# Padding the r and k loads of a fused RWKV-and-FFN kernel to all partitions, with changes to its order of loads and its schedule

## The chip, the cores and the metric

The kernel runs on one core of a Trainium2 chip. The metric is the device time of one execution in microseconds (us), median of several runs. Every run named here was in the fast state (granted TensorE clock 0.98 to 1.00 of full speed on average). A profiled span runs from the first to the last instruction and came out 1 to 2 us below the time of the same run; I compare spans with spans and medians with medians.

Engines: PE is TensorE's matmuls, PEld its weight loads, DVE is VectorE, ACT is ScalarE, POOL is GpSimd, SP issues the loads. All kernel operations go through one helper, so nearly every line of the profile says L91, and tiles are what identifies an operation.

## The reference, cut to what matters

```python
batch, n_heads, seq, head_dim = (4, 8, 768, 48)
for t in range(S):                              # RWKV5, per head
    cur = np.einsum('bhd,bhe->bhde', u[None] * kt, vt)
    y[:, :, t] = np.einsum('bhd,bhde->bhe', rt, state + cur)
    state = w[None, :, :, None] * state + np.einsum('bhd,bhe->bhde', kt, vt)
x = y.transpose(0, 2, 1, 3).reshape(3072, 384)
xn = x / np.sqrt(np.mean(x * x, axis=-1, keepdims=True) + 1e-06) * rms_g
g = xn @ w_gate                                 # 384 x 1536
silu = g * (1.0 / (1.0 + np.exp(-g)))
out = (silu * (xn @ w_val)) @ w_out             # 1536 x 384
```

Everything from `r`, `k` and `v` is float32; the three weight matrices arrive as float64.

## The kernel before

The recurrence is cut into 12 blocks of 64 tokens. In a block, r and k are scaled by powers of w (DVE, "decay"), multiplied into scores (PE), masked, multiplied with v, and added to the state's contribution. The block's output is normalised and goes through the two gated products and the output product. Blocks 0 and 1 use the weights while they are still being loaded as 64-bit pieces (`raw`) and converted by ACT, DVE and POOL into `wa`, `wb`, `wo`. Later blocks run in pairs and need seven products instead of eight for a group, for which sums of weight halves (`s1`, `s2`, `s4`) and of tokens (`t`) must exist.

The tile `chan` (called `CH` in the code) holds r and k of one block with channels in the partitions: two heads of 48 channels, one at rows 0 to 47, one at rows 64 to 111. Only block 0's host array carried the zero rows between them, so all other blocks were loaded in two halves:

```python
def load_chan(s):
    if s == 0:
        sp.dma_start(out=CH, in_=chan_0)
        return
    for z in range(2):
        sp.dma_start(out=CH[64 * z : 64 * z + D], in_=chan[s, z])
```

What happens at the start is laid out by a list scheduler. Each operation is entered with its engine, an estimated cost, and what it reads and writes. A random search over goals picks an order, which every engine then executes as a fixed program. Stretches where PE has nothing to do in the beginning are filled with products of a constant tile (`warm`, called filler below), which are meant to keep PE's clock up. In the trace of this kernel the granted clock is 1.00 in the first 20 us, and 0.50 from 28.6 to 35.4 us, around the end of a gap of 5.73 us in PE's work. The code:

```python
add("DVE", 0.12 + 0.55 * n, ["up"] + keys("CHr"), keys("MEr", "MEt"),
    lambda part=part: decay_r(s, *part), port=True, name=f"R {s}")
...
def warm(us):
    for _ in range(int((us - 0.3) / 0.22)):
        pe.matmul(gv["c"][:, 0, 0:P], ones, ones, start=True, stop=True)

p.run(cells, 25.0, {"PE": 1.5, "DVE": 1.5, "ACT": 3.0, "POOL": 6.3, "SP": 1.7}, warm)
```

The first pair of blocks (2 and 3) makes the remaining sums between its own products; `(m, k)` is the product after which DVE does the add:

```python
if first_block:
    fill.update({(0, 0): lambda: token_sum(s, 3)})
    fill.update({(0, 1): lambda: token_sum(s, 4)})
    fill.update({(1, 0): lambda: unit_sum(1, 1), (2, 0): lambda: unit_sum(2, 1)})
    fill.update({(2, 1): lambda: unit_sum(4, 1), (2, 4): lambda: unit_sum(3, 1)})
```

Of the kernel before, what the change touches and what calls it, by code (L numbers as in the profile page):

```python
# [49 lines left out]
P = 128  # L50
# [10 lines left out]
B, H, S, D = 4, 8, 768, 48  # L61
HP = H // 2
L = 64
NS = S // L
# [29 lines left out]
class Plan:  # L94
# [28 lines left out]
    def schedule(self, goals, free):  # L123
# [34 lines left out]
                    ready[self.ops[j][0]].add(j)  # L158
        return start

    def run(self, cells, first, free, idle=None, trials=3000):



        goals, t = {}, first
        for i in cells:
            goals[i] = t
            t += self.ops[i][1]
        rng, best = random.Random(2), None
        for trial in range(trials):  # L170
            new = dict(goals)
            if trial and rng.random() < 0.5:
                a, by = rng.randrange(len(cells)), rng.uniform(-15, 15)
                for i in cells[a : a + 1 + int(rng.expovariate(1 / 6))]:
                    new[i] += by
            elif trial:
                new[rng.randrange(len(self.ops))] = rng.uniform(0, t)
            start = self.schedule(new, free)
            end = max(start[i] + self.ops[i][1] for i in cells) + 0.3 * sum(start[i] for i in cells) / len(cells)
            if best is None or end <= best[0]:  # L180
                best, goals = (end, start), new
        self.start = best[1]
        busy = free["PE"]
        for i in sorted(range(len(self.ops)), key=lambda i: (self.start[i], i)):
            if self.ops[i][0] == "PE":
                if idle and busy < first:
                    idle(self.start[i] - busy)
                busy = self.start[i] + self.ops[i][1]
            self.ops[i][3]()


@with_exitstack
def fast(ctx, tc, chan, tok, vpad, wka, wkb, wot, cols, u_row, chan_0, out, bad):




# [7 lines left out]
    PIECE = NQ * CC * P  # L205
# [15 lines left out]


    col = c_tile([P, 2 * HP + CC], "col")
    act.dma_start(out=col, in_=cols)
    wraw, ucol, gcol = col[:, 0:HP], col[:, HP : 2 * HP], col[:, 2 * HP :]
    utab = c_tile([P, HP, D], "utab")
    eps = c_tile([P, 1], "eps")
# [85 lines left out]


    def load_chan(s):
        if s == 0:
            sp.dma_start(out=CH, in_=chan_0)
            return
        for z in range(2):
            sp.dma_start(out=CH[64 * z : 64 * z + D], in_=chan[s, z])  # L320

    def load_tok(s):
        sp.dma_start(out=TOK, in_=tok[s])
# [11 lines left out]
    wa = [c_tile([P, NQ, CC, P], f"wa_{i}") for i in range(WQ)]  # L335
    wb = [c_tile([P, NQ, CC, P], f"wb_{i}") for i in range(WQ)]
    wo = [c_tile([P, NQ, DM], f"wo_{i}") for i in range(WQ)]
    CUT, N_RAW, N_BITS = PIECE // 2, 6, 3
    raw_of = [raws.tile([P, CUT], I64, name=f"raw_{i}") for i in range(N_RAW if wide else 0)]
    bits_of = [raws.tile([P, CUT], I32, name=f"bits_{i}") for i in range(N_BITS if wide else 0)]  # L340
    ulp_of = [raws.tile([P, CUT], I32, name=f"ulp_{i}") for i in range(N_BITS if wide else 0)]
# [2 lines left out]
    def piece(p, dst, src, key, lo, size):  # L344



        n = n_pieces[0]
        n_pieces[0] += 1
        flat = free_dims(dst, (1, PIECE))[:, lo : lo + size]  # L350
        part = src[:, lo : lo + size]
        share = size / 576
        if not wide:
            p.add("SP", 0.8 * share, [], [key, "rounded"], lambda: sp.dma_start(out=flat, in_=part), land=2)
            return
        raw, bits, ulp = raw_of[n % N_RAW][:, 0:size], bits_of[n % N_BITS][:, 0:size], ulp_of[n % N_BITS][:, 0:size]
        r, b, u = f"raw{n % N_RAW}", f"bits{n % N_BITS}", f"ulp{n % N_BITS}"
        words = raw.bitcast(I32).rearrange("p (n z) -> p n z", z=2)
        hi, lower = words[:, :, 1], words[:, :, 0].bitcast(U32)
        p.add("SP", 1.35 * share, [], [r], lambda: sp.dma_start(out=raw, in_=part), land=1.8, name=f"load {n}")  # L360
        p.add(
            "ACT", 0.1 + 0.64 * share, [r], [u],
            lambda: act.activation(ulp, lower, AF.Copy, scale=2.0**-29), name=f"ulp {n}",
        )
        p.add(
            "DVE", 0.07 + 0.38 * share, [r], [b],
            lambda: dve.tensor_scalar(
                out=bits, in0=hi, scalar1=3, scalar2=0x3FFFFFF8, op0=ALU.logical_shift_left, op1=ALU.bitwise_and
            ),
            port=True, name=f"bits1 {n}",  # L370
        )
        p.add(
            "DVE", 0.07 + 0.69 * share, [r, b], [b],
            lambda: dve.scalar_tensor_tensor(
                out=bits, in0=hi, scalar=-0x40000000, in1=bits, op0=ALU.bitwise_and, op1=ALU.bitwise_or
            ),
            port=True, name=f"bits2 {n}",
        )
        p.add(
            "POOL", 0.15 + 1.3 * share, [b, u], [key, "rounded"],  # L380
            lambda: pool.tensor_tensor(out=flat.bitcast(I32), in0=bits, in1=ulp, op=ALU.add), port=True,
            name=f"sum {n}",
        )
# [209 lines left out]
    p = Plan()  # L593
# [12 lines left out]
        i = turn["at"] % 2  # L606
        return at[i], f"at{i}"

    add("SP", 0.0, [], ["w"], lambda: None, land=2.4)
    add("DVE", 2.4, ["w"], ["pw"], powers, name="powers")  # L610
    add("DVE", 0.43, ["pw"], ["up"], lambda: dve.tensor_mul(up, pw, by_inv), port=True)
    add("DVE", 0.43, ["pw"], ["down"], lambda: dve.tensor_mul(down, pw_rev, by_inv), port=True)
# [9 lines left out]
    add("ACT", 3.0, ["pw"], ["khd"], state_decay, name="khd")  # L622

    def loads(s):
        add("SP", 2.3 if s == 0 else 1.8, [], ["CHr0", "CHr1", "CHk0", "CHk1"], lambda: load_chan(s), land=1.6)
        add("SP", 1.8, [], ["TOKr", "TOKk"], lambda: load_tok(s), land=1.8)
        add("SP", 1.6, [], ["VSv"], lambda: load_v(s), land=1.8)
        if s == 0:
            add("SP", 0.5, [], ["utab"], load_u, land=1.8)

    def mixing(s):
        quick = s == 0
# [181 lines left out]
    for n, reads, writes in (  # L814
        (1, ["wa2.0", "wa2.1", "wb2.0", "wb2.1"], ["s1"]), (2, ["s1", "wa0.0", "wa0.1", "wa0.2"], ["s2"]),
    ):
        add("DVE", 1.25, ["sums"] + reads, writes, lambda n=n: unit_sum(n, 0), port=True, name=f"sum {n}")
    cell(1, 3)
    for n, reads, writes in (
        (4, ["s2", "wb0.0", "wb0.1", "wb0.2"], ["s4"]), (3, ["wa0.0", "wa0.1", "wa0.2"], ["wa2.0", "wa2.1"]),  # L820
# [10 lines left out]
        for _ in range(int((us - 0.3) / 0.22)):  # L831
            pe.matmul(gv["c"][:, 0, 0:P], ones, ones, start=True, stop=True)

    p.run(cells, 25.0, {"PE": 1.5, "DVE": 1.5, "ACT": 3.0, "POOL": 6.3, "SP": 1.7}, warm)


    def at_bank(name):
# [154 lines left out]
    for s in range(FIRST, NS, 2):  # L992
        first_block, n = s == FIRST, s + 2
        fill = {}
        if first_block:
            fill.update({(0, 0): lambda: token_sum(s, 3)})
            fill.update({(0, 1): lambda: token_sum(s, 4)})
            fill.update({(1, 0): lambda: unit_sum(1, 1), (2, 0): lambda: unit_sum(2, 1)})
            fill.update({(2, 1): lambda: unit_sum(4, 1), (2, 4): lambda: unit_sum(3, 1)})
        if n < NS:  # L1000
            plan = {
                (0, 2): "R", (1, 1): "K", (1, 4): "1", (2, 0): "2", (2, 2): "3d", (3, 0): "h", (3, 2): "D",
                (3, 5): "aAm", (4, 1): "M", (4, 2): "H", (4, 4): "yY", (5, 3): "q",
            }
        else:
            plan = {}
        look = {(m, k) for m in range(NN // 2) for k in (2, 5) if m != 2}
        if first_block:
            look = {(m, k) for m, k in look if k == 5 or m == 4}
        elif n == NS:  # L1010
            look |= {(2, 2), (2, 5), (5, 6)}
        for m in range(NN // 2):
            steps = group(s, m)
            for k, f in enumerate(steps):
                f()
                if (m, k) in fill:
                    fill[m, k]()
                if (m, k) in plan:
                    mix(n, plan[m, k])
                if (m, k) in look:  # L1020
                    check()
        if n == NS:
            break
        mix(n, "uU"), mix(n + 1, "R123")
        project(s, 0, False), mix(n, "r"), mix(n + 1, "KdD")
        project(s, 0, True), mix(n + 1, "aA"), mix(n, "n")
        project(s, 1, False), mix(n + 1, "mMh")
        project(s, 1, True), mix(n + 1, "yYH")
        project(s, 2, False), mix(n + 1, "q")
        project(s, 2, True), mix(n + 1, "r")  # L1030
        project(s, 3, False), mix(n + 1, "n")
        project(s, 3, True), mix(n + 1, "uU")
        for x in (1, 2, 3, 4):
            token_sum(n, x)
# [424 lines left out]
@with_exitstack  # L1459
def program(ctx, tc, fast_args, general_args, w, u, out):  # L1460
    nc = tc.nc
    flags = ctx.enter_context(tc.tile_pool(name="flags", bufs=1))
    bad = flags.tile([1, 1], I32, name="bad")
    chan, tok, vpad, wka, wkb, wot, cols, u_row, chan_0 = fast_args
    n_bad = fast(tc, chan, tok, vpad, wka, wkb, wot, cols, u_row, chan_0, out, bad)
    with tc.If(n_bad > 0):
        rT, kT, k, v, w_gate, w_val, w_out, rms_g = general_args
        general(tc, rT, kT, k, v, w, u, w_gate, w_val, w_out, rms_g, out)
# [67 lines left out]
```

## Time and profile before

| what | value |
|---|---|
| time, median of 3 runs | 663.31 us (663.28 to 663.75) |
| first product with a weight (`first_a<-xa,wa`) on PE | 35.28 us |
| first product of the paired blocks (`a<-xa,wa`) | 162.24 us |
| first product of the last output group (`po`) | 623.41 us |

The three starts cut the span into stages. First the head of the page, with the span and each engine's busy time, share and count of instructions.

```profile
span 662.2 us, 15313 instructions
PE 640.5 (97%) x6534; PEld 506.8 (77%) x6534; DVE 385.9 (58%) x560; ACT 341.0 (52%) x952; POOL 44.6 (7%) x39
```

PE is busy for 97% of the span. That average hides what this PE time is: some of the first 35 us is filler. So the busy share says that PE is the bound, but not that nothing can be saved. The stages in the prediction answer that. The second place with idle PE time is the first paired block. The list of waits from 150 to 205 us shows it (columns: engine and tile that waited, engine and tile waited for, total us, times, longest).

```profile
PE b L91 <- DVE gv L91: 1.9, 3, 1.0
PE a L91 <- DVE h L91: 1.3, 1, 1.3
```

PE waits 3.2 us there, always for DVE, which is where the three adds stood that the change moves.

### The profile page before, as it was taken

How to read it: one execution, taken by the hardware profiler on the slowest of the kernel's cores; microseconds unless marked ns; L12 is line 12 of the kernel's file. 1: busy time of each engine (PE TensorE's matmuls, PEld its weight loads, DVE VectorE, ACT ScalarE, POOL GpSimd, SP SyncE). 2: the span in 40 equal slices, each digit the busy share in tenths (PEclk: the TensorE clock that was granted, in tenths of full speed). 3: DMA queues.
4: the chain of work that ended last, by engine and by line, in shares of the span. 5: the costliest groups of instructions: out<-in, count | busy, mean ns of one | idle time of the engine just before them, and what ended most of it. 6: DMA issues, size and time to landing. Idle time of an engine off the chain costs nothing.

```text
span 662.2 us, 15313 instructions
## 1 busy us (share of the span) xinstructions
PE 640.5 (97%) x6534; PEld 506.8 (77%) x6534; DVE 385.9 (58%) x560; ACT 341.0 (52%) x952; POOL 44.6 (7%) x39
## 2 busy tenths in 40 slices
PE   9699999999989999999999999999999999999996
PEld 8586788786868866888866888866888866788753
DVE  5688688854876653576562577572566571555400
ACT  5388248734354573555673555582555492434400
POOL 3044523200000000000000000000000000000000
PEclk9898999999999999999999999999999999999999
DMA  9688636061205232314333314334323321122111
GB/s 281 154 183 296 192 117 172 1 139 47 63 19 118 83 67 76 91 37 97 112 82 89 81 46 87 103 79 113 73 55 75 112 62 29 38 72 73 54 27 28
DMA packets 20078, 61.61 MB, mean 93 GB/s; under 512 B 3072, under 2 KB 6272, under 8 KB 18816
## 3 DMA queue, kind: packets, MB, share of 16 engines
q1 hardware_dynamic: 19856, 60.53, 34.5%
q8 instruction: 53, 0.87, 0.6%
q14 instruction: 25, 0.20, 0.1%
q10 hardware_dynamic: 144, 0.01, 0.0%
HBM read 55.81 MB, written 4.72 MB: 91 GB/s over the span
## 4 chain that ended last, share of the span: by engine, by line
PE 84%; ACT 6%; DVE 4%; DMA 3%; issue 2%; POOL 0%; SPq 0%; DVEq 0%; ACTq 0%; POOLq 0%
PE po L91 24%; PE b L91 15%; PE a L91 10%; PE c L91 9%; PE first_b L91 5%; PE first_c L91 4%; PE first_a L91 4%; PE at L91 4%; PE py L91 3%; PE pa L91 2%; PE pu L91 2%; DMA chan<-in_chan_dram 2%; ACT MO L91 2%; ACT ME L91 1%; DVE gv L91 1%
## 5 line engine op out<-in xcount | busy, mean ns | idle before, releaser
L91 PE MATMUL po<-wo,h 128*128 128x384 f32 x480 | 159.8, 489 | 0.8 <-DVE bad L91 0.8
L91 PEld LDWEIGHTS po<-wo,h 128*128 128x128 f32 x480 | 90.0, 190 | 60.2 <-PE pc L91 0.8
L91 DVE TENSOR_TENSOR gv<-b,m 128x512 f32<-128x512 f32 x90 | 62.0, 689 | 79.4 <-PE b L91 76.0
L91 ACT ACTIVATE gv<-gv 128x512 f32<-128x512 f32 (+1 forms) x60 | 30.9, 518 | 51.5 <-DVE gv L91 51.5
L91 ACT ACTIVATE ME<-dmask,du 64x64 f32<-64x64 f32 x176 | 43.7, 329 | 12.3 <-DVE du L91 11.9
L91 DVE TENSOR_TENSOR gv<-c,gv 128x512 f32<-128x512 f32 x60 | 41.4, 690 | 14.4 <-PE c L91 13.3
L91 ACT COPY o<-po 128x384 f32<-128x384 f32 x20 | 9.5, 474 | 77.4 <-PE po L91 39.3
L91 PE MATMUL a<-xa,wa 64*128 64x256 f32 x360 | 45.0, 382 | 1.9 <-DVE h L91 1.9
L91 PE MATMUL b<-xa,wa 64*128 64x256 f32 x360 | 44.6, 380 | 1.6 <-DVE gv L91 1.6
L91 ACT ACTIVATE MO<-dmask,du 64x64 f32<-64x64 f32 x176 | 44.4, 334 | 0.4
L91 PE MATMUL b<-t,wb 64*128 64x256 f32 x360 | 44.4, 379 | 0.0
L91 PE MATMUL c<-xb,s 64*128 64x256 f32 x360 | 44.3, 378 | 0.0
L91 PE MATMUL b<-t,s 64*128 64x256 f32 x360 | 44.0, 377 | 0.3 <-DVE gv L91 0.3
L91 PE MATMUL c<-t,s 64*128 64x256 f32 x360 | 43.9, 376 | 0.0
L91 PE MATMUL a<-xb,wb 64*128 64x256 f32 x360 | 43.9, 376 | 0.0
L91 ACT ACTIVATE mag<-again 128x288 f32<-128x288 f32 x48 | 22.1, 461 | 35.9 <-DMA again<-in_wot_dram 14.6
L91 PEld LDWEIGHTS a<-xa,wa 64*128 64x128 f32 x360 | 33.8, 187 | 8.3 <-DVE h L91 4.1
L91 PEld LDWEIGHTS b<-xa,wa 64*128 64x128 f32 x360 | 34.1, 187 | 7.6 <-DVE gv L91 4.0
L91 PEld LDWEIGHTS b<-t,s 64*128 64x128 f32 x360 | 34.8, 187 | 4.6 <-DVE gv L91 0.7
L91 PEld LDWEIGHTS c<-t,s 64*128 64x128 f32 x360 | 34.9, 187 | 4.0
L91 PEld LDWEIGHTS a<-xb,wb 64*128 64x128 f32 x360 | 34.9, 187 | 4.0
L91 PEld LDWEIGHTS b<-t,wb 64*128 64x128 f32 x360 | 34.4, 187 | 4.4 <-DVE gv L91 0.3
(146 smaller groups left out, 1095.8 us busy)
## 6 DMA issues: line engine op xcount, KB each, us to landing
TOK<-in_tok_dram SPq DMA_DIRECT2D x12, 768.0 KB, 4.9
chan<-in_chan_dram SPq DMA_DIRECT2D x22, 384.0 KB, 6.4
VS<-in_vpad_dram SPq DMA_DIRECT2D x24, 336.0 KB, 4.9
raw<-in_wot_dram SPq DMA_DIRECT2D x8, 576.0 KB, 4.1
out_dram<-o SPq DMA_DIRECT2D x48, 96.0 KB, 2.2
again<-in_wka_dram SPq DMA_DIRECT2D x16, 288.0 KB, 3.1
again<-in_wkb_dram SPq DMA_DIRECT2D x16, 288.0 KB, 2.8
again<-in_wot_dram SPq DMA_DIRECT2D x16, 288.0 KB, 2.8
```

The source lines that it names most:

```text
L91: return lambda *args, **kwargs: self.tc.keep_in_program_order(give(*args, **kwargs))
```

## The change

The intent has four parts: load r and k of every block over all 128 partitions; bring the small `col` table and block 0's k ahead of other loads; let the search judge an order with later landing times (`LAND` 2.1 us, a `replay` with longer costs, another seed); and make three of the sums inside the plan instead of in the first paired block. The diff, cut to its core:

```diff
     def load_chan(s):
-        if s == 0:
-            sp.dma_start(out=CH, in_=chan_0)
-            return
-        for z in range(2):
-            sp.dma_start(out=CH[64 * z : 64 * z + D], in_=chan[s, z])
+        sp.dma_start(out=CH, in_=chan[s])
 ...  (host)
-    chan_0 = np.zeros((2, 64) + chan.shape[3:], np.float32)
-    chan_0[:, 0:D] = chan[0]
+    chan = np.pad(chan, [(0, 0), (0, 0), (0, 64 - D)] + [(0, 0)] * 4).reshape((NS, P) + chan.shape[3:])
 ...  (first loads)
-    act.dma_start(out=col, in_=cols)
+    sp.dma_start(out=col, in_=cols)
 ...
         if s == 0:
-            add("SP", 0.5, [], ["utab"], load_u, land=1.8)
+            for i, x in ((1, "k"), (0, "r")):
+                add(
+                    "SP", 1.2, [], [f"CH{x}0", f"CH{x}1"],
+                    lambda i=i: sp.dma_start(out=CH[:, i], in_=chan[s, :, i]), land=LAND, name=f"load {x} {s}",
+                )
 ...  (the search)
-        rng, best = random.Random(2), None
+        rng, best = random.Random(3), None
 ...
-            end = max(start[i] + self.ops[i][1] for i in cells) + 0.3 * sum(start[i] for i in cells) / len(cells)
+            end = self.replay(start, free)
+            end = max(end[i] for i in cells) + 0.3 * sum(end[i] for i in cells) / len(cells)
 ...  (the plan)
+    for n, reads, writes in (
+        (1, ["wa3.0", "wa3.1", "wb3.0", "wb3.1"], ["s1'"]), (2, ["s1'", "wa1.0", "wa1.1"], ["s2'"]),
+        (4, ["s2'", "wb1.0", "wb1.1"], ["s4'"]),
+    ):
+        add("DVE", 1.25, ["sums"] + reads, writes, lambda n=n: unit_sum(n, 1), port=True, name=f"sum {n}'")
 ...  (first paired block)
-            fill.update({(1, 0): lambda: unit_sum(1, 1), (2, 0): lambda: unit_sum(2, 1)})
-            fill.update({(2, 1): lambda: unit_sum(4, 1), (2, 4): lambda: unit_sum(3, 1)})
+            fill.update({(2, 4): lambda: unit_sum(3, 1)})
```

More of the change, by code (lines that the diff above doesn't have):

```diff
@@ L159, in schedule, with replay @@
         return start
+    def replay(self, start, free):
+        free, port, end = dict(free), {"DVE": 0.0, "POOL": 0.0}, [0.0] * len(self.ops)
+        for i in sorted(range(len(self.ops)), key=lambda i: (start[i], i)):
+            e, cost, deps, _, _, locks, _ = self.ops[i]
+            s = max([free[e]] + [end[d] + self.hop(d, i) + (1.0 if self.ops[d][0] == "SP" else 0.05) for d in deps])
+            if locks:
+                s = max(s, port["POOL" if e == "DVE" else "DVE"])
+            free[e] = end[i] = s + cost * (1.0 if e == "PE" else 1.05)
+            if locks:
+                port[e] = end[i]
+        return end
     def run(self, cells, first, free, idle=None, trials=3000):
@@ L192, in fast @@
 @with_exitstack
-def fast(ctx, tc, chan, tok, vpad, wka, wkb, wot, cols, u_row, chan_0, out, bad):
+def fast(ctx, tc, chan, tok, vpad, wka, wkb, wot, cols, u_row, out, bad):
     nc = tc.nc
@@ L337, in fast @@
     wo = [c_tile([P, NQ, DM], f"wo_{i}") for i in range(WQ)]
-    CUT, N_RAW, N_BITS = PIECE // 2, 6, 3
+    CUT, N_RAW, N_BITS, LAND = PIECE // 2, 6, 3, 2.1
     raw_of = [raws.tile([P, CUT], I64, name=f"raw_{i}") for i in range(N_RAW if wide else 0)]
@@ L353, in piece @@
         if not wide:
-            p.add("SP", 0.8 * share, [], [key, "rounded"], lambda: sp.dma_start(out=flat, in_=part), land=2)
+            p.add("SP", 0.7 * share, [], [key, "rounded"], lambda: sp.dma_start(out=flat, in_=part), land=LAND)
             return
@@ L359, in piece @@
         hi, lower = words[:, :, 1], words[:, :, 0].bitcast(U32)
-        p.add("SP", 1.35 * share, [], [r], lambda: sp.dma_start(out=raw, in_=part), land=1.8, name=f"load {n}")
+        p.add("SP", 1.35 * share, [], [r], lambda: sp.dma_start(out=raw, in_=part), land=LAND, name=f"load {n}")
         p.add(
@@ L607, in next_at @@
         return at[i], f"at{i}"
-    add("SP", 0.0, [], ["w"], lambda: None, land=2.4)
+    add("SP", 0.3, [], ["w"], lambda: None, land=1.9)
     add("DVE", 2.4, ["w"], ["pw"], powers, name="powers")
@@ L624, in loads @@
     def loads(s):
-        add("SP", 2.3 if s == 0 else 1.8, [], ["CHr0", "CHr1", "CHk0", "CHk1"], lambda: load_chan(s), land=1.6)
-        add("SP", 1.8, [], ["TOKr", "TOKk"], lambda: load_tok(s), land=1.8)
-        add("SP", 1.6, [], ["VSv"], lambda: load_v(s), land=1.8)
         if s == 0:
-            add("SP", 0.5, [], ["utab"], load_u, land=1.8)
+            for i, x in ((1, "k"), (0, "r")):
[3 more added lines that the diff above has]
+                )
+        else:
+            add(
+                "SP", 2.4, [], ["CHr0", "CHr1", "CHk0", "CHk1"], lambda: load_chan(s), land=LAND, name=f"load chan {s}"
+            )
+        add("SP", 1.8, [], ["TOKr", "TOKk"], lambda: load_tok(s), land=LAND, name=f"load tok {s}")
+        add("SP", 3.2, [], ["VSv"], lambda: load_v(s), land=LAND, name=f"load v {s}")
+        if s == 0:
+            add("SP", 0.5, [], ["utab"], load_u, land=LAND)
     def mixing(s):
@@ L832, in warm @@
             pe.matmul(gv["c"][:, 0, 0:P], ones, ones, start=True, stop=True)
-    p.run(cells, 25.0, {"PE": 1.5, "DVE": 1.5, "ACT": 3.0, "POOL": 6.3, "SP": 1.7}, warm)
+    p.run(cells, 25.0, {"PE": 1.5, "DVE": 1.5, "ACT": 2.5, "POOL": 6.3, "SP": 1.8}, warm)
     def at_bank(name):
@@ L1463, in program @@
     bad = flags.tile([1, 1], I32, name="bad")
-    chan, tok, vpad, wka, wkb, wot, cols, u_row, chan_0 = fast_args
-    n_bad = fast(tc, chan, tok, vpad, wka, wkb, wot, cols, u_row, chan_0, out, bad)
+    chan, tok, vpad, wka, wkb, wot, cols, u_row = fast_args
+    n_bad = fast(tc, chan, tok, vpad, wka, wkb, wot, cols, u_row, out, bad)
     with tc.If(n_bad > 0):
@@ L1505 @@
         "u_row": c(u.reshape(HP, 2, D).transpose(1, 0, 2).reshape(2, HP * D)),
-        "chan_0": chan_0.reshape((P,) + chan.shape[3:]),
         "rT": c(r.transpose(0, 1, 3, 2)),
@@ L1527 @@
             tc,
-            [args[n] for n in ("chan", "tok", "vpad", "wka", "wkb", "wot", "cols", "u_row", "chan_0")],
+            [args[n] for n in ("chan", "tok", "vpad", "wka", "wkb", "wot", "cols", "u_row")],
             [args[n] for n in ("rT", "kT", "k", "v", "w_gate", "w_val", "w_out", "rms_g")],
```

## The prediction

> **What bounds the kernel now.** I read the stages first: busy time of each engine in stretches of the span. Columns are stretch, then busy us and instructions of PE, PEld, DVE, ACT, POOL, then granted clock, DMA share and GB/s.
>
> ```profile
> 0.00:10.00 10.00, 8.84 (x85) 8.65 (x86) 3.41 (x22) 4.51 (x10) 5.16 (x13) 1.00 0.82 220
> 10.00:20.00 10.00, 9.31 (x212) 8.52 (x214) 9.71 (x15) 6.09 (x16) 0.00 (x0) 1.00 1.06 329
> 20.00:30.00 10.00, 4.27 (x40) 3.94 (x35) 4.29 (x8) 2.69 (x7) 0.21 (x1) 0.93 0.49 110
> ...
> 160.00:200.00 40.00, 36.79 (x373) 30.86 (x373) 28.69 (x40) 19.43 (x58) 0.00 (x0) 1.00 0.18 44
> 200.00:300.00 100.00, 99.81 (x1046) 78.55 (x1044) 58.32 (x82) 53.31 (x155) 0.00 (x0) 1.00 0.32 78
> ```
>
> From 60 to 155 us, and from 200 us on, PE has no gap worth having (99.8 of 100 us): the bound there is PE work, which the change leaves as it is. Only two places hold recoverable time: the start, where no weight product can run before the first token block is ready (the first `first_a<-xa,wa` starts at 35.28 us; much of the PE time before it is filler on `ones`), and 160 to 200 us, where PE lacks 3.2 us. Whatever the start loses, the end loses, since PE is full afterwards.
>
> Next the timeline of 20 to 31 us (start, duration, what, idle before and its releaser).
>
> ```profile
> 21.98 1.58 PE L91 MATMUL first_c<-ones 128*128 128x128 f32 x12
> 25.79 1.22 DVE L91 TENSOR_TENSOR ME<-chan,up 128x1024 f32<-128x1024 f32 x1 [5.24 <-DMA chan<-in_chan_dram]
> ...
> 27.10 1.04 ACT L91 COPY MO<-ME 64x1024 f32<-64x1024 f32 x1 [5.52 <-DVE ME L91]
> ...
> 28.17 0.26 ACT L91 ACTIVATE ms<-at,eps 128x2 f32<-128x2 f32 x1
> 28.46 0.17 DVE L91 RECIPROCAL ms<-ms 128x2 f32<-128x2 f32 x1
> 28.66 0.48 DVE L91 TENSOR_SCALAR diag<-ident,ms 128x128 f32<-128x128 f32 x2
> ...
> 29.29 1.19 PE L91 MATMUL at<-diag,ones 128*128 128x256 f32 x2 [5.73 <-DVE diag L91]
> ...
> 30.52 0.95 DVE L91 TENSOR_TENSOR xa<-yT_first,at 128x768 f32<-128x768 f32 x1 [0.91 <-PE at L91]
> ```
>
> The normalisation of block 0 needs nothing from block 1, but on ACT its square root (28.17) stands behind the copy of block 1's r, and on DVE its reciprocal stands behind block 1's decay. Both therefore wait for block 1's `chan` load. The chain of work that ended last says how long that load took, and which load started everything:
>
> ```profile
> 0.81 6.14 DMA col<-in_cols_dram
> ...
> 14.98 10.68 DMA chan<-in_chan_dram
> ```
>
> Last, what the DMA engines moved in 15 to 17 us (full-height weight loads) and in 19 to 21 us (the 48-row `chan` load):
>
> ```profile
> DMA packets 295, 0.81 MB, mean 404 GB/s; under 512 B 32, under 2 KB 32, under 8 KB 295
> ```
>
> ```profile
> DMA packets 57, 0.34 MB, mean 172 GB/s; under 512 B 12, under 2 KB 12, under 8 KB 17
> ```
>
> DMA is about 100% busy in both, at 404 and 172 GB/s (142 in 21 to 23 us). Same engines, less than half the rate: rows reached, not bytes, set the time.
>
> [...] block 0's `chan` (1 MB, 2.6 us at 404 GB/s) took 5.9 us to land, interleaved with others. [...]after PE's 5.73 us gap the granted clock is 0.50 in 30 to 35 us.
>
> **The change part by part.**
>
> *Order.* Comparing the built programs, DVE, ACT and POOL have the same compute order until about 58 us of the old time (ACT only loses the issue of `col`), and PE swaps only a filler and two weight products. The new random search alters the order from there to the end of the plan, where PE was full before. So the start changes through the data's arrival times.
>
> *First loads.* `col` (5.5 KB) goes from ACT's queue, where its packets shared engines with 1 MB of `chan` and landed at 6.96, to the head of SP's queue. [...]Then k, then r, half of `chan` each: at 404 GB/s about 1.3 us apiece, landing about 5 and 6.3 (the whole was in by 6.8 before). DVE's powers took 6.98 to 9.78 until `up` was ready; now about 3.5 to 6.3, so the first decay starts near 6.4 against 9.81: DVE gains about 3 us. ACT gains about 2 (its k copies start at 5 against 6.98), and hands block 0's scores to PE about 1.7 us sooner. DVE then ends its `KH` pair near 17.5 against 20.55. Alone this is worth nothing: DVE would just wait longer for `chan`.
>
> *Block 1's load.* In the new SP order it stands behind four raw weight pieces, not six (2 x 393 KB less, 1.95 us at 404 GB/s). Before, its bytes started to flow at about 17.4, so now at 15.4. It carries 1.05 MB, not 0.79[...]: 2.6 us at 404 GB/s, to 18.0[...]: 19.8 against 25.66. That is later than the 17.5 where DVE is free, so DMA remains the releaser with some 2 us of wait, and the gain here is 25.79 - 19.8 = **6.0 us**.
>
> *From there to the first weight product.* Decay, copy, root, reciprocal, diag and spread take the same durations, so the first `xa` starts near 24.5 minus half a microsecond. PE's gap shrinks to about 3 us (its filler ends some 3 us sooner, the spread comes 6 us sooner), so its clock may stay up: the spread then takes about 0.6, not 1.19, and the 64 state matmuls 1.6, not 2.80. Since ACT has to evict them before its 8 us of diagonals, I add **1.0 us** (0 if the clock falls, 1.5 if it holds throughout). Block 1's tok data come right behind: 18.0 + 1.95 for two pieces + 1.95 = 21.9, landed by 24, just in time. After this, compute follows compute (ACT diagonals, conversion, silu), and the whole stretch to 58 us moves with it. Sum at the start: **7.0 us**.
>
> *Sums of the other half.* Three adds of 1.34 us leave groups 0 to 2 of the first paired block. There DVE is in arrears: PE waited 1.02 (after `s<-s,wa` and TOK), 1.32 (diagonals late because `du` stood behind `s<-wb,s`), 0.30 and 0.57 us, together 3.2. One of four adds, into `wa`, stays. I give back 2.8 of the 3.2. In the plan the adds fall into 120 to 160 us, where DVE is busy 23.5 of 40 us; in 140 to 160 only 8 of 20. I charge 0.3 for a product delayed by one. Net **2.5 us**.
>
> *Later loads.* The other `chan` loads save a DMA issue each and move a third more bytes, but were hidden: PE is 99.8% busy there. Worth 0.
>
> Sum: 7.0 + 2.5 = 9.5; 663.3 - 9.5 = **653.8 us**, 1.4% faster.
>
> **The rivals.** (1) *The start gains the full DVE head start and more.* If the padded load lands by 17.5, the gain is 8.3 + 1.5 us, and with 3.2 us from the sums 13.0: 650.3, barely under 2%. For it: full-height pieces ran at 404 GB/s. Against: the DMA engines are full from 2 to 17 us, and five more loads stand ahead. (2) *A new wait takes over.* The load comes early, but tok, or the raw pieces now behind `chan`, arrive late (padding adds 262 KB a block, 0.65 us), or ACT becomes the limit; then the start gives 3 to 4 us and the total is near 657.5. For it: tok has only 1 us to spare by my sum. Against: two raw pieces, 0.79 MB, now follow `chan` instead of preceding it, and the padding adds only a third of that. (3) *The new order costs PE.* A product placed before its converted weights or behind the three adds would open gaps in 60 to 155 us, where there were none; 2 to 3 us back, near 656. For it: the old order left no gap to win. Against: DMA is only 0.36 to 0.76 busy there in the old run. (4) *All was hidden*: 663. Against it: PE is full right after.
>
> **Range and chances.** Rivals 1 and 2 bound the range: 650.4 to 657.6. Faster by 2% needs 650.0, which takes every favourable term at once: 0.09. Slower by 2% needs 13 us lost, and no part adds so much to PE: 0.01. Within 2%: 0.90.
>
> **What would show it.** Right: `ME<-chan,up` of 1024 elements starts near 20 with a DMA wait of 1 to 4 us; 17 to 19 us moves about 400 GB/s; `col` lands before 4.5; first `first_a<-xa,wa` near 28 (35.28 before); first paired `a<-xa,wa` 6 to 8 us before 162.24; PE lacks under 1 us in the 40 us after that. Wrong: the spread still waits over 5 us, so the DMA rate was not the cause; or the first product comes early but the paired stage does not, so a gap opened between; or PE's wait in the paired block stays, so the adds were not the cause.

The sum stands: 7.0 us at the start (6.0 at the decay of block 1, 1.0 behind it) and 2.5 us from the adds, together 9.5, so 653.8 us. Terms behind two of its numbers, those that put `col` at 3.5 us, and the one that leads block 1's load from 18.0 to 19.8 us, on which the 6.0 rests, were my estimates and were not shown, as is the like step of tok from 21.9 to "landed by 24". The 404 GB/s set for the padded load is what full-height pieces did in the trace. That the clock may stay up over a gap of about 3 us was a guess as well: the only gap for which the prediction gives a clock is that of 5.73 us.

## The result, and the profile after

The changed kernel takes **655.0 us** (median of 4 fast runs, 654.23 to 656.65) against 663.29 (4 fast runs, 662.28 to 663.75) of the kernel before. The ratio is 0.988, with a 95% interval of 0.9858 to 0.9903. A ratio in this document is the mean time of one kernel's fast runs over that of the other's of the same rounds, so it is not quite the ratio of the medians quoted. The change is a gain of 1.2%; the interval leaves out both no gain and a gain of 2%.

Head of the page, after:

```profile
span 653.1 us, 15289 instructions
PE 638.6 (98%) x6534; PEld 504.7 (77%) x6534; DVE 384.7 (59%) x560; ACT 341.9 (52%) x952; POOL 41.7 (6%) x39
```

PE has the same number of recorded instructions, and only 1.9 us less busy time, while the span fell by 9.1. Most of the gain is therefore time in which PE had been idle. Three of the stages after, in the same columns as in the prediction:

```profile
20.00:30.00 10.00, 9.24 (x150) 8.31 (x148) 9.12 (x16) 6.85 (x18) 1.40 (x2) 1.00 0.70 221
...
160.00:200.00 40.00, 38.94 (x400) 33.74 (x398) 28.02 (x43) 18.43 (x55) 0.00 (x0) 1.00 0.21 65
200.00:300.00 100.00, 99.81 (x1046) 78.54 (x1044) 57.80 (x81) 55.55 (x161) 0.00 (x0) 1.00 0.28 83
```

Between 20 and 30 us PE was busy for 4.27 us before and is for 9.24 us now, DVE for 4.29 and now 9.12. From 160 to 200 us PE went from 36.79 to 38.94. From 200 us on nothing changed. These are the two places that the prediction named. The timeline of 20 to 28 us shows the first of them:

```profile
20.58 1.23 DVE L91 TENSOR_TENSOR ME<-chan,up 128x1024 f32<-128x1024 f32 x1 [0.27 <-DMA chan<-in_chan_dram]
...
21.90 1.04 ACT L91 COPY MO<-ME 64x1024 f32<-64x1024 f32 x1 [0.55 <-DVE ME L91]
...
24.09 0.67 PE L91 MATMUL at<-diag,ones 128*128 128x256 f32 x2 [0.76 <-DVE diag L91]
24.80 0.95 DVE L91 TENSOR_TENSOR xa<-yT_first,at 128x768 f32<-128x768 f32 x1 [0.39 <-PE at L91]
...
25.81 1.64 PE L91 MATMUL at<-VS,KH 128*48 128x48 f32 x64
...
27.38 1.57 PE L91 MATMUL first_a<-xa,wa 64*128 64x256 f32 x12
```

The decay of block 1 starts 5.2 us earlier (25.79 before), and DVE waits 0.27 us for its load instead of 5.24. The wait of PE before the spread (`at<-diag,ones`) shrank from 5.73 to 0.76 us, the two spreads take 0.67 and not 1.19 us, and the 64 state matmuls 1.64 and not 2.80, since the clock does not fall in this stretch: the granted clock is 1.00 from 16 to 36 us after, and was 0.50 from 30 to 35 us before. (Later, from about 47.5 to 51 us, it does fall to 0.50 in this run, and the 12 products `first_b<-wo,hbuf` there take 5.81 us; in after_again, the same kernel, they take 4.12, and that run is only 0.3 us shorter.) The chain of work that ended last has the load of block 1 as one piece (start, duration):

```profile
14.81 5.65 DMA chan<-in_chan_dram
```

It is issued at 14.81 us, within 0.3 us of the two halves before, and takes 5.65 us, where the second half took 10.68. What the DMA engines moved from 17 to 19 us, when it is in flight:

```profile
DMA packets 111, 0.82 MB, mean 411 GB/s; under 512 B 7, under 2 KB 7, under 8 KB 13
```

It moves at 411 GB/s, where the load in two halves moved at 172. The padded load is also one transfer instead of two, but the trace before speaks against that as the cause: each raw piece there is a transfer of its own, of the same 393 KB as a half, over all rows, and they moved at 404 GB/s. So the rows covered are what the traces show to count: 404 and 411 GB/s over 128 rows, 142 to 172 over 48. By what mechanism, no trace shows.

Not everything went as well. The timeline of 1 to 13 us shows what became of the earlier first loads:

```profile
1.16 8.40 PE L91 MATMUL first_c<-ones 128*128 128x128 f32 x50 [1.16 <-DVE pw L91]
...
9.49 1.15 PE L91 MATMUL first_a<-chan,hbuf 48*64 48x64 f32 x32
...
12.42 0.69 DVE L91 TENSOR_TENSOR ME<-first_a,dmask 64x512 f32<-64x512 f32 x1 [2.95 <-PE first_a L91]
```

The inputs of block 0's first scores are ready sooner (ACT starts on k at 4.93 us, 6.98 before), but the scores stand behind filler products that last until 9.5 us. They start at 9.49; before, they started at 8.85. DVE, which had gained 3 us, then waits 2.95 us for them.

The last view for now is the list of waits of 150 to 200 us, after, with the same two pairs of engines as before:

```profile
PE b L91 <- DVE gv L91: 0.9, 2, 0.6
PE a L91 <- DVE h L91: 0.2, 1, 0.2
```

PE's 3.2 us of waiting for DVE in the first paired block became 1.1 us.

By stage, from the two profiled runs: the first weight product comes 7.90 us earlier, block 1's spread (52 us) 6.48 us earlier, the first paired product 6.48 us earlier, and the last output group 9.15 us earlier. So the start gave 6.5 us, of the 7.9 it had first won 1.4 were lost before 52 us, the rest of the plan gave nothing, and the first paired block gave 2.7.

### The profile page after: what moved, and what is told of

The parts are those of the page before. It is cut to its first block, busy times and chain, and to the rows that moved or that the text cites. A ratio compares the mean times of both kernels' runs of the same rounds, so it can differ in the third digit from the quotient of the medians.

```text
span 653.1 us, 15289 instructions
## 1 busy us (share of the span) xinstructions
PE 638.6 (98%) x6534; PEld 504.7 (77%) x6534; DVE 384.7 (59%) x560; ACT 341.9 (52%) x952; POOL 41.7 (6%) x39
## 4 chain that ended last, share of the span: by engine, by line
PE 86%; DVE 5%; ACT 4%; issue 2%; DMA 1%; POOL 0%; DVEq 0%; ACTq 0%; POOLq 0%; SPq 0%
PE po L91 24%; PE b L91 15%; PE a L91 10%; PE c L91 9%; PE first_c L91 5%; PE first_b L91 5%; PE first_a L91 5%; PE at L91 4%; PE py L91 4%; PE pa L91 2%; PE pu L91 2%; ACT ME L91 1%; DVE TOK L91 1%; ACT MO L91 1%; DVE gv L91 1%
## 5 line engine op out<-in xcount | busy, mean ns | idle before, releaser
L91 PEld LDWEIGHTS c<-xb,s 64*128 64x128 f32 x360 | 34.5, 187 | 4.1
```

The source lines that it names most:

```text
L91: return lambda *args, **kwargs: self.tc.keep_in_program_order(give(*args, **kwargs))
```

## The experiments

The theory to be tested: (a) the padded load of block 1 gives most of the gain, by covering all 128 rows; (b) the place of that load in SP's order gives the rest of the start; (c) the moved adds give about 2.5 us; (d) the early `col`, the padded loads of later blocks and the new order in the plan give nothing. The main rival for (a) and (b) is that the start improved because the first loads were reordered or because the filler kept the clock up, whatever the shape of the load. In the expectations, R 1 and K 1 are the decay of block 1's r and k on DVE, inv 0 the reciprocal and x 0 the `xa` of block 0, as the plan names them. In each kernel one thing is changed (the last ones join edits), and the order of every engine is otherwise the same as in its parent. All runs gave correct results. The kernel before: medians of 11 runs each 663.07, 662.57 and 663.03 us, on different chips, so kernels are compared by their ratios.

**after_again** is the changed kernel once more, without an edit, as the base.

> The changed kernel again, as the yardstick for the other runs of this chip. Expected 654 to 656 us against 663.3, ratio 0.987 to 0.989; in its profile the second block's decay on DVE starts near 20.6 us, the closing spread of the second block near 52 us, the first paired product near 155.8 us.

Measured 654.36 us (654.2 to 654.89), ratio 0.9872 (0.9857 to 0.9886). The stages repeat within half a microsecond: first paired product at 155.46, last output group at 613.98.

**unpad_1** gives block 1 alone its two 48-row halves again.

```diff
     def load_chan(s):
+        if s == 1:
+            for z in range(2):
+                sp.dma_start(out=CH[64 * z : 64 * z + D], in_=chan[s, 64 * z : 64 * z + D])
+            return
         sp.dma_start(out=CH, in_=chan[s])
```

> Only block 1's load of r and k is cut back into two halves of 48 rows; the order of every engine is the same as in the changed kernel. [...]the halves move at 140 to 170 GB/s, so the load lands 2.5 to 4 us later (near 23.5 instead of 20.5), the second block's decay starts there, PE's gap before the spread grows to about 4 us or more, and the end comes 3 to 4.5 us later: 658 to 659.5 us. Rival, that the load came early only because two raw pieces no longer stand ahead of it: landing within 1 us of 20.5 and under 1 us more in total.

Measured 659.18 us (658.3 to 661.19), ratio 0.9949. That one load costs 4.8 us, with less to move. Its decay in the timeline, and then the DMA engines from 17 to 19 us:

```profile
24.04 1.23 DVE L91 TENSOR_TENSOR ME<-chan,up 128x1024 f32<-128x1024 f32 x1 [4.52 <-DMA chan<-in_chan_dram]
```

```profile
DMA packets 60, 0.33 MB, mean 166 GB/s; under 512 B 15, under 2 KB 15, under 8 KB 22
```

The wait is back at 4.52 us and the rate at 166 GB/s, with the DMA engines as busy as before (their queue took 101% of 16 engines' time from 17 to 19 us, and 104% from 19 to 21 us in the kernel before). PE has a gap of 3.28 us again, from 24.27 to 27.55, and its clock is 0.50 from 22 to about 32 us (mean 0.60 from 20 to 30 us, 0.78 from 30 to 35). The gap didn't start this fall, as two stages show (the clock is the third number from the right):

```profile
20.00:22.00 2.00, 1.73 (x15) 1.73 (x16) 0.00 (x0) 1.38 (x5) 0.00 (x0) 0.99 0.92 193
22.00:24.00 2.00, 2.00 (x11) 1.97 (x10) 0.00 (x0) 0.00 (x0) 0.00 (x0) 0.50 1.05 365
```

By these means the clock fell just before 22 us (estimate), about 2.3 us before the gap, when PE had been busy for 1.73 of the last 2.00 us. So not all of the 4.8 us is the load: its decay starts 3.5 us later than in the changed kernel, and the runs of unpad_1 with the highest mean clock (0.994 and 0.993) took 658.3 and 658.4 us, those with the lowest (0.988) 661.0 and 661.2. Padding this load is worth about half of the change's gain of 8.7 us, and the rival falls as its explanation, since the first loads and the filler were those of the changed kernel.

**before_pad** does the same from the other side: the kernel before, with only the padded loads.

```diff
     def load_chan(s):
         if s == 0:
             sp.dma_start(out=CH, in_=chan_0)
             return
-        for z in range(2):
-            sp.dma_start(out=CH[64 * z : 64 * z + D], in_=chan[s, z])
+        sp.dma_start(out=CH, in_=chan[s])
 ...  (host)
-        "chan": chan,
+        "chan": np.pad(chan, [(0, 0), (0, 0), (0, 64 - D)] + [(0, 0)] * 4).reshape((NS, P) + chan.shape[3:]),
```

> The kernel before with nothing changed but padded loads of r and k over all 128 rows for blocks 1 to 11; its order stays. [...]block 1's load still starts to flow near 17.4 us behind six raw pieces, takes 2.6 us instead of 5 and more, and lands near 22 instead of 25.7; the first xa comes 3.5 to 4.5 us earlier, the total is 659 to 660 us. Rival, that only the order of loads matters: under 1 us gained.

Measured 658.88 us (658.51 to 659.51), ratio 0.994 (0.9921 to 0.9958): 3.7 us between the medians. In its profile the decay of block 1 starts at 22.06 us after a wait of 1.23, PE's gap is 1.73 us with the clock at 1.00, and the first paired product starts at 157.19, 5.05 us before that of the kernel before. From there to the last output group it takes 461.50 us against 461.17: the paired part is unchanged, as it should be.

**chan_after6** keeps the padding, but puts the load of block 1 behind six raw pieces, as in the kernel before, instead of four.

```diff
         self.start = best[1]
+        at = {op[6]: i for i, op in enumerate(self.ops)}
+        self.start[at["load chan 1"]] = self.start[at["load 5"]] + 1e-6
```

> The changed kernel with block 1's load of r and k moved behind all six raw weight pieces, where the kernel before had it. My prediction's term: two pieces of 393 KB more in front cost about 1.95 us, so the load lands near 22 instead of 20.5 and the total is 655.8 to 656.6 us (654.4 to 655 for the changed kernel). Rival: the engines had room (their share fell to 0.3 at 16 to 17 us in the changed kernel, since the load was issued only at 14.8), so the two pieces fill a gap and cost under 0.7 us.

Measured 657.4 us (655.95 to 659.54), ratio 0.9908 (0.9883 to 0.9933). The decay of block 1 starts at 21.78 us, only 1.2 later, but the first paired product starts at 158.71, 3.0 us later than in the changed kernel's first profile. The total was expected at 655.8 to 656.6 us, so the later place cost more than the prediction's term. (The share of 0.3 at 16 to 17 us in the expectation is 0.41 in the stages of the changed kernel.) Two stages of the profile show a fall of the clock:

```profile
24.00:26.00 2.00, 0.71 (x4) 0.69 (x5) 1.53 (x7) 0.40 (x2) 0.21 (x1) 1.00 0.00 0
26.00:28.00 2.00, 2.00 (x22) 1.77 (x22) 1.97 (x3) 1.16 (x2) 0.79 (x1) 0.59 0.60 135
```

PE waited 2.27 us for the diagonals, and after that its clock was 0.59 from 26 to 28 us and 0.55 from 28 to 30, where the state matmuls took 2.63 us, not 1.64. The clock fell a second time, to 0.63 to 0.69, from 45 to 55 us. So the later place costs 1.2 us of landing in the trace; that the falls of the clock make up the whole of the rest is my reading of the stages, and not isolated by a run. The single runs agree with it: the one with a mean clock of 0.996, as high as in after_again (0.996 to 0.997), took 655.95 us, the profiled one with 0.991 657.72, and the one with 0.989 659.54.

**unpad_late** gives blocks 2 to 11 their two halves again (`if s >= 2:` in the edit of unpad_1).

> The changed kernel with the loads of r and k of blocks 2 to 11 cut back to halves of 48 rows; block 1 stays padded. Theory: they are all hidden, so 0 us, at most 0.5: 654.3 to 655.3. Rival: block 2's slow load (issued near 33 us, in the stretch where DMA is full) holds up the raw pieces behind it, or the slow loads delay the re-reads of the weights later: 1 us or more.

Measured 654.32 us (654.0 to 655.83), ratio 0.9871, the same as the changed kernel's. Ten of the eleven padded loads are worth nothing, because these loads are hidden.

**col_act** puts `col` back on ACT's queue.

```diff
-    sp.dma_start(out=col, in_=cols)
+    act.dma_start(out=col, in_=cols)
```

> Only the small load of w, u and gains goes back to ACT's queue. My theory after seeing the result: in the changed kernel DVE has its powers ready early but then waits 2.95 us for the first score products, which stand on PE behind 25 filler products until 9.5 us; so an early col is worth nothing, and this costs 0 to 0.5 us: 655 to 655.5. Rival, the step of my prediction: the early col carries the gain of the DVE chain, and its loss costs 2 to 3 us.

Measured 654.14 us (653.71 to 654.85), ratio 0.9868. `col` landed at 4.55 us and not at 6.96 as in the kernel before. The load beside it is half as large here (0.52 MB; beside 1.05 MB in before_pad it landed at 7.26), but that this is the cause was not isolated. So only 2.1 us of the earliness were taken back. The decay of block 1 still started at 20.33. Those 2.1 us are worth nothing. Had `col` come as late as before, the answer might differ; that was not run.

**sums_back** gives the three adds back to the first paired block, with empty slots in the plan, so that the order stays.

```diff
-        add("DVE", 1.25, ["sums"] + reads, writes, lambda n=n: unit_sum(n, 1), port=True, name=f"sum {n}'")
+        add("DVE", 1.25, ["sums"] + reads, writes, lambda: None, port=True, name=f"sum {n}'")
 ...
-            fill.update({(2, 4): lambda: unit_sum(3, 1)})
+            fill.update({(1, 0): lambda: unit_sum(1, 1), (2, 0): lambda: unit_sum(2, 1)})
+            fill.update({(2, 1): lambda: unit_sum(4, 1), (2, 4): lambda: unit_sum(3, 1)})
```

> Only the three adds go back from the plan to groups 1 and 2 of the first paired block, at the places of the kernel before; the plan's order is otherwise the same. Theory: PE's waits of about 3.2 us come back there (1.0, 1.3, 0.3, 0.6 us) against 1.05 now, and the end comes 2.2 to 2.8 us later: 657.3 to 657.8. Rival, that the gain after 160 us comes from the padded loads of later blocks or from another order: under 0.7 us more.

Measured 656.77 us (656.46 to 657.57), ratio 0.9909: 2.4 us more than after_again. PE's waits from 150 to 200 us are word for word the two lines shown for the kernel before, 3.2 us in all. From the first paired product to the last output group it takes 461.09 us, against 458.52 of after_again. The adds are the cause, and giving them to the plan cost nothing that can be seen.

**filler16** tests what the start still loses: it lets `warm` make at most 16 products, where the first gap had 25, so that the scores are not held up.

```diff
-        for _ in range(int((us - 0.3) / 0.22)):
+        for _ in range(min(int((us - 0.3) / 0.22), 16)):
```

> The changed kernel with 16 instead of 25 filler products before the first scores. Theory that PE's filler holds the scores back: the first score product starts near 6.8 instead of 9.5, block 1's load is issued near 12.4 instead of 14.8 and lands near 19, the first xa comes 1.3 to 2.2 us earlier than in the changed kernel, and the total is 653 to 654 us. Rival, that the DMA engines set the landing whatever the issue: under 0.5 us gained. Second rival: less filler leaves PE's clock low at the scores, and the gain goes there.

Measured 654.74 us (654.35 to 655.48), ratio 0.9879: no gain. The first scores start at 6.97 us and not at 9.49, and the `KH` pair on DVE ends at 18.04 and not at 20.31, so the head start does reach DVE. But then DVE waits for the load again:

```profile
20.16 1.23 DVE L91 TENSOR_TENSOR ME<-chan,up 128x1024 f32<-128x1024 f32 x1 [2.12 <-DMA chan<-in_chan_dram]
```

The load was issued at 12.69 us, 2.1 sooner, and took 7.35 instead of 5.65 us; it landed 0.4 us sooner. Issued that early, the load finds its landing set by what stands ahead of it in the DMA queue (one piece less there is worth 0.75 us, see filler16_after3 below). (In the changed kernel itself the DMA engines were only 0.41 busy from 16 to 17 us, against 1.05 here, so there the issue still counted, for about these 0.4 us.) I had expected a gain, and that expectation fell. So did the second rival: the first 32 score products take 1.15 us, as in the changed kernel, and show no lower clock.

**root_first** lets ACT do block 0's root, and DVE its reciprocal, diagonals and `xa`, before the decay of block 1, so that they no longer wait for block 1's load.

```diff
         self.start = best[1]
+        at = {op[6]: i for i, op in enumerate(self.ops)}
+        self.start[at["R 1"]] = self.start[at["inv 0"]] + 1e-6
+        self.start[at["Rc 1"]] = self.start[at["inv 0"]] + 2e-6
+        self.start[at["K 1"]] = self.start[at["x 0"]] + 1e-6
```

> The changed kernel with block 1's decay of r (DVE) and its copy (ACT) moved behind block 0's reciprocal, and block 1's decay of k behind block 0's scaling. Block 0's normalisation then waits for no load. DVE is nearly full from 12.4 to 29 us in the changed kernel, so only the two decays' 2.4 us are swapped: first xa about 1.1 us earlier, but du, after which ACT's diagonals start, at the same time; total 0.3 to 1.2 us less, 654 to 654.7. Rival: nothing, because du and not xa starts ACT's chain.

Measured 654.04 us (653.55 to 654.74), ratio 0.987. `xa` comes 1.5 us sooner (23.22), the first weight product at 25.18, but PE then waits 2.0 us for POOL's conversion of `wa`, and the first paired product starts at 154.62, 0.8 us before that of after_again. The difference in time is within the intervals.

**filler16_root** joins the two edits.

> Both edits, less filler and the root first. DVE is then done with block 0 near 17.5, and the root needs no load: first xa near 22 instead of 24.8, du near 26 instead of 28.6; total 2 to 3.5 us less than the changed kernel, 651.5 to 653. Rival, that the two gains do not add because the load of block 1 remains the bound: no better than less filler alone.

Measured 653.54 us (652.9 to 655.02), ratio 0.9864 (0.9841 to 0.9886). First paired product at 154.07 us; PE's wait for POOL's `wa` is 2.0 us again. The 2 to 3.5 us expected did not come. Inconclusive as to time.

**filler16_after3** is filler16 with one raw piece fewer ahead of block 1's load.

```diff
+        at = {op[6]: i for i, op in enumerate(self.ops)}
+        self.start[at["load 3"]] = self.start[at["load chan 1"]] + 1e-6
```

> 16 filler products as before, and one raw piece fewer ahead of block 1's load. Less filler alone had the load issued 2.1 us earlier and landing at the same 20.1 us, so what stands ahead on the DMA engines set the landing. If so, one piece of 393 KB less brings the landing to about 19.1 and the second block's decay with it; total 0.7 to 1.0 us below less filler alone, 653.5 to 654. Rival, that the load itself takes that long: still landing near 20.

Measured 654.39 us (652.9 to 656.1), ratio 0.9865. The decay starts at 19.41, 0.75 us before that of filler16: one piece less in the queue is worth 0.75 us of landing, which again says that the queue sets it. The time hardly follows (653.5 to 654 was expected), and the interval (0.9842 to 0.9888) holds no change at all.

**best_try** puts together what each of these showed: short filler, root before the decay, the decay of k behind the bonus, one raw piece fewer ahead.

```diff
-        for _ in range(int((us - 0.3) / 0.22)):
+        for _ in range(min(int((us - 0.3) / 0.22), 16)):
 ...
+        self.start[at["R 1"]] = self.start[at["inv 0"]] + 1e-6
+        self.start[at["Rc 1"]] = self.start[at["inv 0"]] + 2e-6
+        self.start[at["K 1"]] = self.start[at["bonus3 1"]] + 1e-6
+        self.start[at["load 3"]] = self.start[at["load chan 1"]] + 1e-6
```

> Attempt at a better version: less filler, root first, one raw piece fewer ahead, and block 1's decay of k behind du. First xa near 22, du near 25.7 to 26.5 instead of 27.8 at its end, ACT's diagonals from about 27.4 instead of 29.9; total 652.5 to 653.5. Rival: the chain from 28 to 52 us hangs on conversions of weights (DVE, POOL), not on xa and du, and nothing more comes: 653.5 to 654.

Measured **652.74 us** (652.07 to 653.56), ratio 0.9841 (0.9818 to 0.9864), the best of all. The decay of block 1 in its timeline:

```profile
20.99 1.22 DVE L91 TENSOR_TENSOR ME<-chan,up 128x1024 f32<-128x1024 f32 x1
```

The decay waits for nothing any more, the first weight product starts at 26.20 us (24.59 in filler16_root; here the clock was 0.50 from about 21.1 to 24.5 us, an estimate from its means of 0.77, 0.50 and 0.76 in 20 to 22, 22 to 24 and 24 to 25 us, although PE's longest gap before that, once begun, was 0.54 us), the first paired product starts at 153.12 and the last output group at 611.63. It beats the kernel before clearly. Against the changed kernel it is about 1.6 us ahead by medians, and all its runs are below all of that kernel's; but the intervals of the ratios touch (0.9818 to 0.9864 against 0.9857 to 0.9886), so this smaller gain is likely rather than settled.

## Why the prediction was right or wrong

The total was predicted as 653.8 us and is 655.0, inside the range; the class was right as well. Taken by its steps:

1. *Two places hold recoverable time.* Right. The stages from 200 us on are the same to 0.01 us of PE time in 100, and the whole gain of 9.15 us falls before 52 us (6.48) and in the first paired block (2.67).
2. *The rows reached set the load's time.* Right, shown from both sides: unpad_1 takes the rate from 411 down to 166 GB/s and costs 4.8 us, before_pad gains 3.7 to 5.0. Landing was put at 19.8 us and is 14.81 + 5.65 = 20.46.
3. *Fewer raw pieces ahead of the load.* The mechanism was right, the size was off. The step "2 x 393 KB less, 1.95 us" measured 1.2 us of landing in chan_after6, and one piece 0.75 us in filler16_after3. The step also lacked the clock: in the profiled run the later place opened a gap of 2.27 us in PE, the clock fell to 0.50 some 1.1 us after it (estimate from the mean of 0.69 from 26 to 27 us), and 3.0 us were lost instead of 1.2.
4. *The first loads.* `col` was put at 3.5 us and landed at 2.43 (1.6 us after its issue at the head of SP's queue; it took 6.1 us before, on ACT's queue, where 98 of its packets moved from 3 to 5 us along with 98 of SP's); the first decay was put at 6.4 and started at 6.63. The step that failed is "hands block 0's scores to PE about 1.7 us sooner", and with it "ends its `KH` pair near 17.5". The scores started 0.64 us later and the pair ended at 20.31, because I had taken PE to be free when the inputs came, although 25 filler products stood ahead of the scores in PE's fixed program. The sum didn't suffer, since the prediction had given this head start no value of its own. filler16 confirms that: once the scores run early, DVE waits 2.12 us for the load and gains 0.4.
5. *A wait of 1 to 4 us for the load remains.* Wrong: 0.27 us. DVE arrived late (step 4) just as the load landed a little later than predicted. The gain at the decay was 5.2 and not 6.0 us.
6. *The clock stays up and gives 1.0 us.* Right in kind, the size is larger: the first weight product came 7.90 us earlier, 2.7 more than the decay. Of these, 0.5 are the shorter spread, 1.1 the filler products behind it (1.28 us, 2.34 before) and 1.2 the shorter state matmuls. The step had left the filler out. It starts at 27.38, where "near 28" was predicted. The clock was 1.00 from 20 to 30 us in all five traces with this start (after, after_again, col_act, sums_back, unpad_late), and in that of after up to 36 us.
7. *"The whole stretch to 58 us moves with it."* This failed in part: of 7.90 us, 6.48 were left at block 1's spread. The step took the chain to go on from the first weight product's side, by way of the state matmuls and ACT's diagonals, as it did before. In the chain of work that ended last after the change (start, duration), the stretch behind the spread goes over DVE instead, from `xa` to `du` and the conversions, to POOL's conversion of `wa`:

```profile
27.65 0.95 DVE du L91
...
38.49 1.84 POOL wa L91
```

The same conversion stands at 45.01 us in the chain before, so it came 6.52 us earlier: what PE gained from shorter state matmuls was not all on the path any more. PE also waits 1.05 us for a weight of POOL at 32.23, a new wait, and 2.0 us in root_first, but this wait is not in the chain. This is rival 2 in small. Which DVE operation holds the chain was not isolated by a run.

8. *The adds are worth 2.5 us.* Right: 2.4 by medians and 2.6 in the profiles of sums_back against after_again. PE lacks 1.06 us in the 40 us after the first paired product, a shade more than the "under 1 us" predicted.
9. *The new order in the plan is worth nothing* (rival 3 would cost 2 to 3 us). Right in the sum: 6.48 us at 52 us and 6.48 at 156. *Later loads are worth nothing.* Right: unpad_late. One reading in rival 3 is wrong: from 60 to 155 us the DMA share before is not 0.36 to 0.76, but 0.00 to 1.05 in stretches of 5 us. Nothing rested on it.

The sum of start and adds was 7.0 + 2.5 and came out as 6.48 + 2.67 in the profiled runs; by medians the gain is 8.3 us, somewhat less than the 9.2 between those two runs. That the start came so near is in part luck: against the 7.0, the decay gave 0.8 us less, the way from there to the first weight product 1.7 more, and 1.4 were lost behind it. The parts also overlap. Taken away one at a time, the padding costs 4.8 us, the place in the queue about 2.4 (estimate from the ratios 0.9908 and 0.9872) and the adds 2.4, together more than the 8.7 us that the whole change gained, and in the profiles of the first two the clock fell as well.

## What to carry to other kernels

Where loads and a fixed program meet, read the landing of a load from what stands ahead of it in the queue (one raw piece less: 0.75 us sooner in filler16_after3) and from how many rows it covers (411 GB/s over 128 rows, 142 to 172 over 48); a load that is larger but covers all partitions can land earlier (1.05 MB at 20.46 us, where 0.79 MB in halves landed at 23.92 in unpad_1), and only the one that something waits for is worth the effort. An input that arrives early is worth nothing if its consumer stands behind filler or behind another wait in its engine's order, so follow each gain to the engine that must use it. A gap in PE can cost more than its length, because the products after it may run at half the clock: at 0.50, behind the gap of 5.73 us in the kernel before, the 64 state matmuls took 2.80 us, and 1.64 at 1.00 after the change. But the gap's length alone did not decide it here. The clock fell after a gap of 2.27 us (chan_after6) and stayed at 1.00 after 2.37 us (filler16) and 1.73 us (before_pad), and it also fell where PE had hardly a gap (unpad_1, busy for 1.73 of the 2.00 us before; best_try, longest gap 0.54 us). So look at the granted clock itself and at several runs before giving time to a gap.
